# Attention and two feed-forward layers on one core: bank turns in the planner, offsets to the keys by section, zero products early

## The chip, the cores and the metric

One NeuronCore of a Trainium2 chip runs the whole program in one launch. The metric is device microseconds of that launch, the median of several runs. Five engines work side by side, each through its own list of instructions in order: TensorE (PE, matmuls), VectorE (DVE), ScalarE (ACT), GpSimd (POOL) and SyncE (SP), which here issues all DMA transfers.

## The reference

Attention within blocks of 64 tokens, then two feed-forward layers over 2304 tokens (512 to 2048 to 512 features each):

```python
def _attn_ref(q, k, v):          # (4, 8, 576, 64), chunks of 64
    scores = scale * np.matmul(q_c, k_c.transpose(0, 1, 2, 4, 3))
    scores = scores - np.max(scores, axis=-1, keepdims=True)
    attn = np.exp(scores)
    attn = attn / (np.sum(attn, axis=-1, keepdims=True) + 1e-09)
    return np.matmul(attn, v_c)
def _moe_ref(x, w_in, w_out, s, b):
    r = np.maximum(x @ w_in, 0.0)
    return (s * (r * r) + b) @ w_out
def _moe2_ref(x, w_in, w_out):
    h = x @ w_in
    return (np.maximum(h, 0.0) + np.log1p(np.exp(-np.abs(h)))) @ w_out
```

The weights arrive as float64, the rest as float32.

## The kernel before

**The stages.** (1) Attention over 18 tiles of 128 tokens by 512 features. (2) The first layer's input product, in 24 "quads": each is a 2 by 2 block product done with seven multiplications (p1 to p7, in the manner of Strassen and Winograd), for eight pairs of weight rows and three groups of six tiles. (3) The first layer's output product in six blocks of 16 steps. (4) The second layer's input product, again 24 quads. (5) Its output product, by the seven forms of the same scheme (`second_by_blocks`). All operands are split into a high and a low part (ACT makes the high part, DVE the low one), and each product is three matmuls of 384 columns: high by high, high by low, low by high.

**One tile of attention** (`attention`): DMAs of q, k in two halves, and v; scores on PE (L743) into a bank of kind `at`; the row maximum on DVE (L757); for the first six tiles the exponential on ACT in eight pieces with their sums (L767, after a negation at L779), for the others a subtraction on DVE (L789), one exponential on ACT (L802) and a sum on DVE (L810); a reciprocal on DVE (L820, L821); a multiplication on POOL (L827); turns on PE (L843); a copy out of the bank by ACT or DVE (L360, L362); values on PE (L862); then the result's forms, split into high and low (L515 on ACT, L524 on DVE), with subtractions on DVE and POOL (L502).

**A quad** (`quad`): p1, p6, p7 and p5 accumulate one after the other in one bank `ba`; between them ACT copies the partial sum as a seed into the banks of p2, p4 (`seed`, L948), ACT or DVE copies it out, and DVE subtracts (L502). So p6 waits for ACT's seed after p1, p7 for the copy after p6, and p5 for two readers of the same bank after p7, ACT's seed and DVE's subtraction. ACT finishes each output with L958. Products are L926.

**A block** (`block`, L1104): each of 16 steps has four accumulators (d = 0 to 3), each with three matmuls; the step's high and low parts lie in one of NGH = 4 buffers, so the split for step m+4 waits until all four accumulators of step m are done.

**Weights** come as float64 and are converted by `convert`: a DMA, five steps on DVE (L410, L440, L454, L468, L482) and one on ACT (L427) per half.

**What sets the order.** The program is first recorded as a list of `Op`s, each with the engines that may do it and their costs, a key (its due time in the author's scale), what it depends on, and which `Place`s (banks, buffers) it uses. `Work.order` then plays the list through: at each step it takes the engine and the operation that can start first and, among those that can start within 0.02, the one with the smallest key. What may go to two engines goes to the one that is found so. The instructions are written out in that order, and each engine executes its part strictly in it; semaphores between engines keep the dependences. PSUM has eight banks: two of kind `A`, three `S`, three `at`.

**The opening.** Before the planned list, DVE makes a zero tile, and five products of it (L1417) run on PE into the banks A and S.

## Time and profile before

| | |
|---|---|
| median of 3 runs | 820.55 us (819.38 to 821.25) |
| profiled execution | 818.22 us |
| its span, first to last instruction | 816.4 us |
| mean granted clock of PE | 0.993 of full |
| DMA | 180 MB, 221 GB/s on average |

The page gives busy shares of the engines over the span; as matmuls overlap one another, a busy PE need not run at its peak. The views by stretch tell how the shares change along the program: attention and the first quads lie in the first 100 us, the first layer's remaining quads up to about 258, the blocks up to about 460 with the first quads of the second layer from about 420, the quads up to about 630, and `second_by_blocks` from there to 812. In a timeline a row is one or more like instructions, with its start, its duration, the engine, the line and the tiles; in brackets stands the idle time of that engine just before it, and what ended it. A tile's name with its number left out (`at`, `S`, `last`) is a bank or a buffer of that kind.

### The profile page before, as it was taken

The page shows a single profiled execution, that of the slowest core. Times are in us where ns is not written, and L with a number is a line of the kernel's source. Part 1 is how long each engine was busy: PE and PEld are TensorE (multiplying, and loading weights), DVE is VectorE, ACT ScalarE, POOL GpSimd, SP SyncE. Part 2 cuts the span into 40 slices and gives each one's busy share as a digit, 9 for nine tenths or more (in the row PEclk, how much of TensorE's full clock was granted, in tenths as well). Part 3 has the DMA queues.
Part 4 walks back from the last instruction along what each step waited for, and adds up shares of the span by engine and source line. Part 5 has one row for each costly group of instructions (what it writes and reads, how often), then busy time and mean ns, then how long its engine had stood idle before and what let it go on. Part 6 is the DMA issues. An engine that isn't in the chain of part 4 may idle for free.

```text
span 816.4 us, 14526 instructions
## 1 busy us (share of the span) xinstructions
PE 788.6 (97%) x5117; PEld 771.9 (95%) x5117; DVE 637.4 (78%) x1170; ACT 507.4 (62%) x1080; POOL 144.7 (18%) x162
## 2 busy tenths in 40 slices
PE   5788999999999999999999999999999999999998
PEld 4677899999998999999999999999999999999997
DVE  5799899988856998989856696879675777777864
ACT  4655766666658796666566675565555565655543
POOL 4334422111110222222212230212010000000000
PEclk9799999999999999999999999999999999999999
DMA  8675368779759766778520037766778987678851
GB/s 246 202 200 170 127 188 285 240 244 286 241 192 349 287 226 199 257 218 256 199 83 35 15 141 265 240 230 206 280 237 268 348 351 245 220 255 285 265 193 59
DMA packets 80633, 180.27 MB, mean 221 GB/s; under 512 B 9008, under 2 KB 53040, under 8 KB 79664
## 3 DMA queue, kind: packets, MB, share of 16 engines
q1 hardware_dynamic: 80560, 179.34, 66.3%
q8 instruction: 40, 0.66, 0.3%
q14 instruction: 33, 0.27, 0.1%
HBM read 111.15 MB, written 68.16 MB: 220 GB/s over the span
## 4 chain that ended last, share of the span: by engine, by line
PE 88%; DVE 5%; ACT 2%; DMA 2%; issue 1%; SPq 1%; POOL 0%; DVEq 0%; ACTq 0%; POOLq 0%
PE at L926 19%; PE S L926 12%; PE S L1104 9%; PE at L1104 9%; PE S L1256 8%; PE at L1256 8%; PE A L926 8%; PE A L1104 6%; PE A L1256 5%; PE at L862 1%; DVE operands L524 1%; SPq L377 1%; PE at L743 1%; DVE mem L502 1%; DMA last<-in_k_dram 1%
## 5 line engine op out<-in xcount | busy, mean ns | idle before, releaser
L502 POOL TENSOR_TENSOR mem<-mem 128x256 f32<-128x256 f32 x120 | 109.7, 924 | 377.4 <-DVE mem L482 300.8
L524 DVE TENSOR_TENSOR operands<-mem,operands 128x384 fp32r<-128x384 f32 (+4 forms) x186 | 126.0, 698 | 53.9 <-ACT operands L515 52.2
L515 ACT CAST operands<-mem 128x384 fp32r<-128x384 f32 (+4 forms) x186 | 111.2, 620 | 59.2 <-PE at L1256 36.2
L524 DVE TENSOR_TENSOR operands<-last,operands 128x384 fp32r<-128x384 f32 (+2 forms) x184 | 111.2, 617 | 43.2 <-ACT operands L515 35.7
L515 ACT CAST operands<-last 128x384 fp32r<-128x384 f32 (+2 forms) x184 | 94.4, 527 | 75.7 <-PE A L1104 48.7
L926 PE MATMUL at<-operands 128*128 128x384 f32 x624 | 121.7, 337 | 0.2 <-ACT S L948 0.2
L926 PEld LDWEIGHTS at<-operands 128*128 128x128 f32 x624 | 109.6, 188 | 1.2 <-ACT S L948 1.1
L1104 PE MATMUL S<-operands 128*128 128x384 f32 x432 | 90.7, 335 | 1.2 <-ACT operands L515 0.9
L1104 PE MATMUL at<-operands 128*128 128x384 f32 x432 | 90.3, 334 | 0.0
L1256 PE MATMUL at<-operands 128*128 128x384 f32 x384 | 87.2, 334 | 0.0
L1256 PE MATMUL S<-operands 128*128 128x384 f32 x384 | 87.2, 334 | 0.0
L926 PE MATMUL S<-operands 128*128 128x384 f32 x420 | 82.7, 337 | 1.4 <-ACT S L948 1.4
L1104 PEld LDWEIGHTS S<-operands 128*128 128x128 f32 x432 | 76.2, 188 | 1.8 <-ACT operands L515 1.2
L958 ACT ACTIVATE mem<-S 128x384 f32<-128x384 f32 x104 | 51.1, 491 | 42.3 <-PE S L926 39.5
L1104 PEld LDWEIGHTS at<-operands 128*128 128x128 f32 x432 | 76.3, 188 | 0.0
L926 PEld LDWEIGHTS S<-operands 128*128 128x128 f32 x420 | 73.4, 188 | 1.8 <-ACT S L948 1.7
L1256 PEld LDWEIGHTS at<-operands 128*128 128x128 f32 x384 | 68.4, 188 | 0.0
L1256 PEld LDWEIGHTS S<-operands 128*128 128x128 f32 x384 | 68.4, 188 | 0.0
L502 DVE TENSOR_TENSOR mem<-mem 128x384 f32<-128x384 f32 (+1 forms) x108 | 59.4, 571 | 9.9 <-ACT mem L958 9.1
L926 PE MATMUL at<-last,operands 128*128 128x384 f32 x336 | 66.7, 336 | 0.5 <-ACT S L948 0.2
L1104 PE MATMUL A<-operands 128*128 128x384 f32 x288 | 65.3, 334 | 0.0
L926 PE MATMUL A<-operands 128*128 128x384 f32 x300 | 60.3, 340 | 1.1 <-ACT S L948 0.9
(79 smaller groups left out, 1199.9 us busy)
## 6 DMA issues: line engine op xcount, KB each, us to landing
mem<-in_w_dram SPq DMA_DIRECT2D x64, 512.0 KB, 4.6
summed<-mem SPq DMA_DIRECT2D x168, 192.0 KB, 2.4
mem<-summed SPq DMA_DIRECT2D x30, 768.0 KB, 5.0
hid<-mem SPq DMA_DIRECT2D x96, 192.0 KB, 3.7
last<-hid SPq DMA_DIRECT2D x24, 768.0 KB, 4.5
last<-summed SPq DMA_DIRECT2D x12, 768.0 KB, 5.2
mem<-forms SPq DMA_DIRECT2D x7, 1024.0 KB, 7.4
last<-in_q_dram SPq DMA_DIRECT2D x18, 256.0 KB, 4.2
```

Of the source, the lines that this page charges most:

```text
L377: lambda e: nc.sync.dma_start(out=out(), in_=in_()),
L502: lambda e: on(e).tensor_tensor(out=out(), in0=x(), in1=y(), op=op or ALU.subtract),
L515: lambda e: nc.scalar.copy(out=hi().bitcast(F32R), in_=x()),
L524: lambda e: nc.vector.tensor_tensor(out=lo().bitcast(F32R), in0=x(), in1=hi(), op=ALU.subtract),
L743: nc.tensor.matmul(out_[c * D : (c + 1) * D, pr], of("q")[:, pr * P + c * D : pr * P + (c + 1) * D], kb[:, :, pr, c, :], start=True, stop= ...
L862: nc.tensor.matmul(at(px)[y, x], of("v")[y, x], of("aT")[y, x], start=True, stop=True)
L926: nc.tensor.matmul(acc(dst)().rearrange("p (u c) -> p u c", u=GROUP), l[a], r[c], start=start and kk == 0 and x == 0, stop=kk == 1 and x == 2,
L958: lambda e: nc.scalar.activation(out=at(go), in_=acc(place)(), func=AF.Softplus if ph else AF.Relu),
L1104: nc.tensor.matmul(at(accs[d])[:, :N], l[a], r[c], start=m == 0 and z == 0, stop=m == NM - 1 and z == 2,)
L1256: nc.tensor.matmul(at(accs[d])[:, :N], l[a], r[c], start=i == 0 and y == 0, stop=i == NF - 1 and y == 2,)
```

## The change

`TUNE` is a table of 167 numbers that are added to the keys: by section and its turn ("block0 0 1 10": block, even step, group 0, half 1, step 10) and by the operation's place in a section ("attention.3": its fourth operation). `begin` names the section at each start. In `Work.order` an operation that uses a bank may not start before the last user of that bank, on another engine, has ended and handed over. Some costs are new (exponentials 0.3 instead of 0.4 a piece, scores 0.95 instead of 1.07), and the time up to which PE is counted at half speed goes from 16.25 to 7. `warmed` fills the gaps that PE has in the played-through order, up to the first use of the third S bank, with products of a zero tile `nought`, 512 columns each, into that bank; nobody reads them. There are 74 of them.

```diff
@@ TUNE, Place, Work @@
+TUNE = {
+    "attention 1": 3.5, "attention 14": 87, "attention 15": 11, "attention 16": -14, "attention 3": 6,
...
+}
-        self.kind, self.index, self.left = kind, None, 0
+        self.kind, self.index, self.left, self.last = kind, None, 0, None
+    BANKS = "A", "S", "at"
-    COLD = 16.2532
+    COLD = 7.0
+    def begin(self, part, *turn):
+        self.part, self.turn, self.nth = part, " ".join(map(str, (part, *turn))), 0
@@ add @@
+        kind, self.nth = f"{self.part}.{self.nth}", self.nth + 1
+        key += TUNE.get(self.turn, 0.0) + TUNE.get(kind, 0.0)
@@ order @@
+            for u in op.gives:
+                if u.kind in self.BANKS and u.last and u.last[1] != e:
+                    t = max(t, u.last[0] + self.AFTER[u.last[1]] + self.BEFORE[e])
...
+                u.last = op.end, e
+    IDLE = 0.22
+    def warmed(self, done, emit, kind, index):
+        t, out, unused = 0.0, [], True
+        for op in done:
+            unused = unused and all((u.kind, u.index) != (kind, index) for u in op.takes)
+            if op.on == "PE" and unused:
+                for x in range(int((op.start - t) / self.IDLE / (2 if op.start < self.COLD else 1))):
+                    out.append(Op({"PE": self.IDLE}, 0, [], [], [], emit, 0))
...
+                t = op.end
+            out.append(op)
+        return out
@@ attention, block (and the same in the other sections) @@
+        work.begin("attention", t)
-        o1 = add({"PE": 1.07}, key, scores, loads, [sc], r=sp("q", "k"))
+        o1 = add({"PE": 0.95}, key, scores, loads, [sc], r=sp("q", "k"))
-            o5 = add({"ACT": 8 * 0.4}, key, exps, [o3], [sc, *own], w=sp("e"))
+            o5 = add({"ACT": 8 * 0.3}, key, exps, [o3], [sc, *own], w=sp("e"))
+            work.begin(f"block{m % 2}", j, half, m)
@@ the end of the kernel @@
+        nc.vector.tensor_copy(out=nought, in_=zero[:, :P])
-        for op in done:
+        def idle(e):
+            x = bank["S"][2].rearrange("p (a b) -> p a b", b=P)
+            nc.tensor.matmul(x, nought, nought.unsqueeze(1).to_broadcast([P, KK, P]), start=True, stop=True)
+        for op in work.warmed(done, idle, "S", 2):
             op.emit(op.on)
```

What each engine is given to do is otherwise the same: the same products, splits, conversions and DMAs. Of the copies that may go to ACT or DVE, those of 512 columns are 12 on DVE and 18 on ACT before, 6 and 24 after.

The list of SP at the start, before (q, k, v and w are the inputs; k comes in two halves; `last_120` is the tile buffer of attention, `mem` the one for raw weights):

```order
L377 DMA last_120<-in_q_dram 128x512
L377 DMA last_120<-in_k_dram 64x512 x2
L377 DMA last_120<-in_v_dram 128x512
L377 DMA mem<-in_w_dram 128x1024 x2
L377 DMA last_120<-in_q_dram 128x512
L377 DMA last_120<-in_k_dram 64x512 x2
L377 DMA last_120<-in_v_dram 128x512
L377 DMA last_120<-in_q_dram 128x512
L377 DMA last_120<-in_k_dram 64x512 x2
```

and now (L446 is the load's line in the changed kernel):

```order
L446 DMA last_121<-in_q_dram 128x512
L446 DMA last_121<-in_k_dram 64x512 x2
L446 DMA mem<-in_w_dram 128x1024
L446 DMA last_121<-in_q_dram 128x512
L446 DMA last_121<-in_k_dram 64x512 x2
L446 DMA last_121<-in_q_dram 128x512
L446 DMA last_121<-in_k_dram 64x512 x2
L1405 DMA s_sb<-in_s_dram 128x1
L1406 DMA b_sb<-in_b_dram 128x1
L446 DMA mem<-in_w_dram 128x1024
L446 DMA last_121<-in_v_dram 128x512
```

The second half of the weights and v of the first tile went behind q and k of three tiles.

The list of PE at the start, before (`S_69` is the third S bank; L743 scores, L843 turns, L862 values):

```order
L1417 MATMUL S_69<-operands 128x512
L743 MATMUL at_70<-last_120 64x128 x8
L743 MATMUL at_71<-last_120 64x128 x8
L743 MATMUL at_72<-last_120 64x128 x8
L843 MATMUL at_70<-ident,last_120 128x128 x4
L862 MATMUL at_70<-last_120 64x64 x16
L743 MATMUL at_71<-last_120 64x128 x8
```

and now (L815, L915 and L934 are the same three, L1502 the zero products):

```order
L1498 MATMUL S_69<-operands 128x512
L1502 MATMUL S_69<-nought 128x512 x9
L815 MATMUL at_70<-last_121 64x128 x8
L1502 MATMUL S_69<-nought 128x512 x7
L815 MATMUL at_71<-last_121 64x128 x8
L1502 MATMUL S_69<-nought 128x512 x3
L815 MATMUL at_72<-last_121 64x128 x8
L1502 MATMUL S_69<-nought 128x512 x8
L915 MATMUL at_70<-ident,last_121 128x128 x4
L1502 MATMUL S_69<-nought 128x512 x4
L815 MATMUL at_71<-last_121 64x128 x8
L934 MATMUL at_70<-last_121 64x64 x16
```

Zero products stand between nearly all of the early steps, and the fourth scores went ahead of the first values.

The list of PE at the start of the first layer's blocks, before, where the last product of the quads (L926) is followed by the round of four accumulators (L1104), which then repeats to the end of the block:

```order
L926 MATMUL A_66<-operands 128x384 x6
L1104 MATMUL S_68<-operands 128x384 x3
L1104 MATMUL S_67<-operands 128x384 x3
L1104 MATMUL at_70<-operands 128x384 x3
L1104 MATMUL A_65<-operands 128x384 x3
L1104 MATMUL S_68<-operands 128x384 x3
```

and now, some twenty operations into the first block (L1179; x12 is one accumulator over four steps):

```order
L1179 MATMUL A_65<-operands 128x384 x9
L1179 MATMUL S_68<-operands 128x384 x3
L1179 MATMUL A_65<-operands 128x384 x3
L1179 MATMUL S_68<-operands 128x384 x9
L1179 MATMUL S_69<-operands 128x384 x12
L1179 MATMUL at_71<-operands 128x384 x12
L1179 MATMUL A_65<-operands 128x384 x3
L1179 MATMUL S_68<-operands 128x384 x3
```

The round is gone: one accumulator runs ahead over several steps, and the others follow it.

## Rows read from the trace of the kernel before

**Rows 1.** The page, part 1: busy time, share of the span, instructions.
```profile
PE 788.6 (97%) x5117; PEld 771.9 (95%) x5117; DVE 637.4 (78%) x1170; ACT 507.4 (62%) x1080; POOL 144.7 (18%) x162
```

**Rows 2.** Busy time of each engine by stretches of 40 us, columns as named.
```profile
core 0: us, PE busy (x) PEld busy (x) DVE busy (x) ACT busy (x) POOL busy (x), PEclk, DMA share, GB/s
0.00:40.00 40.00, 25.67 (x291) 20.55 (x293) 26.53 (x59) 23.09 (x109) 15.45 (x25) 0.87 0.75 222
40.00:80.00 40.00, 35.06 (x533) 30.01 (x530) 39.03 (x79) 22.75 (x39) 17.93 (x20) 1.00 0.67 194
80.00:120.00 40.00, 39.27 (x355) 37.04 (x354) 35.78 (x65) 29.05 (x58) 15.45 (x16) 1.00 0.46 147
...
320.00:360.00 40.00, 40.00 (x232) 40.00 (x232) 35.07 (x67) 26.87 (x55) 10.20 (x12) 1.00 0.76 238
```

**Rows 3.** Timeline, block loop: start, duration, engine, line, operation [idle before it <-releaser].
```profile
420.72 0.68 PE L1104 MATMUL A<-operands 128*128 128x384 f32 x3
...
421.24 1.20 PE L1104 MATMUL S<-operands 128*128 128x384 f32 x6
421.43 0.51 ACT L515 CAST operands<-last 128x384 fp32r<-128x384 f32 x1 [1.57 <-PE A L1104]
421.98 0.56 DVE L524 TENSOR_TENSOR operands<-last,operands 128x384 fp32r<-128x384 f32 x1 [1.52 <-ACT operands L515]
```

**Rows 4.** Timeline of PE after attention, places with waits.
```profile
90.98 1.15 PE L862 MATMUL at<-last 64*64 64x64 f32 x32
...
95.95 1.32 PE L926 MATMUL A<-operands 128*128 128x384 f32 x6 [0.50 <-ACT S L948]
...
466.47 1.32 PE L926 MATMUL S<-operands 128*128 128x384 f32 x6 [1.39 <-ACT S L948]
...
501.92 1.31 PE L926 MATMUL at<-last,operands 128*128 128x384 f32 x6 [0.19 <-ACT S L948]
```

**Rows 5.** Timeline of PE in the first 28 us.
```profile
3.26 1.48 PE L1417 MATMUL S<-operands 128*128 128x512 f32 x3
...
5.47 1.97 PE L743 MATMUL at<-last 128*64 128x128 f32 x16 [0.73 <-DMA last<-in_k_dram]
...
11.45 1.98 PE L743 MATMUL at<-last 128*64 128x128 f32 x16 [4.00 <-DMA last<-in_k_dram]
...
14.17 1.98 PE L743 MATMUL at<-last 128*64 128x128 f32 x16 [0.74 <-DMA last<-in_k_dram]
...
19.05 1.09 PE L743 MATMUL at<-last 128*64 128x128 f32 x16
...
24.41 1.97 PE L743 MATMUL at<-last 128*64 128x128 f32 x16
```

**Rows 6.** Stretches of 2 us, with the granted clock.
```profile
24.00:26.00 2.00, 2.00 (x26) 1.86 (x22) 0.86 (x3) 1.87 (x13) 1.57 (x2) 0.50 0.81 259
```

**Rows 7.** Timeline of ACT, pieces of the exponentials of tiles 0, 2 and 5.
```profile
9.08 0.30 ACT L767 ACTIVATE last<-at,mx 128x64 f32<-128x64 f32 x1
...
11.11 0.34 ACT L767 ACTIVATE last<-at,mx 128x64 f32<-128x64 f32 x1
...
22.41 0.36 ACT L767 ACTIVATE last<-at,mx 128x64 f32<-128x64 f32 x1
...
35.59 0.35 ACT L767 ACTIVATE last<-at,mx 128x64 f32<-128x64 f32 x1
```

**Rows 8.** Timeline of DVE, two of the reciprocals.
```profile
37.46 0.20 DVE L821 RECIPROCAL sm<-sm 128x8 f32<-128x8 f32 x1
...
86.53 0.20 DVE L821 RECIPROCAL sm<-sm 128x8 f32<-128x8 f32 x1
```

**Rows 9.** DVE's instructions by form: busy us, mean ns, idle before.
```profile
L482 DVE SCALAR_TENSOR_TENSOR mem<-mem 128x512 f32<-128x512 f32 x64 | 43.9, 686 | 1.2
...
L362 DVE COPY last<-at 128x512 f32<-128x512 f32 x6 | 4.1, 678 | 0.1
```

**Rows 10.** Timeline of ACT, a seed.
```profile
253.50 0.46 ACT L948 COPY S<-at 128x384 f32<-128x384 f32 x1 [0.26 <-DVE mem L502]
```

More of the change, by code (lines that the diff above doesn't have):

```diff
@@ L113 @@
     BYTES = 300e3
-    COLD = 16.2532
+    COLD = 7.0
     def __init__(self):
         self.ops = []
+        self.part, self.turn, self.nth = "", "", 0
+    def begin(self, part, *turn):
+        self.part, self.turn, self.nth = part, " ".join(map(str, (part, *turn))), 0
     def add(self, engines, key, emit, deps=(), uses=(), size=0, after=()):
+        kind, self.nth = f"{self.part}.{self.nth}", self.nth + 1
+        key += TUNE.get(self.turn, 0.0) + TUNE.get(kind, 0.0)
         op = Op(engines, key, [d for d in deps if d is not None], [], list(uses), emit, size)
@@ L133, in add @@
             u.left += 1
+        op.kind, op.turn = kind, self.turn
         self.ops.append(op)
@@ L205, in order @@
         return done
+    IDLE = 0.22
[6 more added lines that the diff above has]
+                    out.append(Op({"PE": self.IDLE}, 0, [], [], [], emit, 0))
+                    out[-1].on, out[-1].start = "PE", t + x * self.IDLE
+                    out[-1].end = out[-1].start + self.IDLE
+                t = op.end
+            out.append(op)
+        return out
 def dve(n, fast=False, pointers=0, port=True):
@@ L277, in block_attention_two_layers @@
         ident = const.tile([P, P], F32, name="ident")
+        nought = const.tile([P, P], F32R, name="nought")
         s_sb = const.tile([P, 1], F32, name="s_sb")
@@ L534, in weights1 @@
     def weights1(ph, i, key):
+        work.begin("weights1", ph, i)
         wf, wp = Place("wf"), Place("w1")
@@ L552, in weights2 @@
     def weights2(ph, i, key):
+        work.begin("weights2", ph, i)
         x = ((AT_XO, 3) if ph == 0 else (AT_S2, 1))
@@ L843, in turned @@
                 nc.tensor.transpose(at(pt)[:, c], of("e")[:, c], ident)
-        o8 = add({"PE": 0.44}, key, turned, [o7], [pt, *own], r=sp("e"))
+        o8 = add({"PE": 0.48}, key, turned, [o7], [pt, *own], r=sp("e"))
         o9 = add(
@@ L866, in attention @@
         key += 0.3
-        o10 = add({"PE": 1.07}, key, values, [o9, load_v], [px], r=sp("aT", "v"))
+        o10 = add({"PE": 1.05}, key, values, [o9, load_v], [px], r=sp("aT", "v"))
         got = lambda: two(at(px))
@@ L889, in forms_held @@
     def forms_held(u, key):
+        work.begin("held", u)
         (xe, ce), (xd, cd) = held[2 * u], held[2 * u + 1]
@@ L905, in quad @@
     def quad(ph, i, j, w, keys, kinds):
+        work.begin(f"quad{ph}", i, j)
         wp, w_done = w
@@ L1142, in forms_of @@
     def forms_of(j, key):
+        work.begin("forms_of", j)
         spans = [(ybuf[2 * j + x], KK4) for x in range(2)]
@@ L1154, in second_by_blocks @@
     def second_by_blocks(ph, t0):
+        work.begin("second", "start")
         V2, G2, GH = 512, 4 * N, 2 * N
@@ L1168, in weights @@
         def weights(n, key, gone=None):
+            work.begin("weights", n)
             wp = Place("w1")
@@ L1227, in second_by_blocks @@
             for i in range(NF):
+                work.begin(f"second{i % 4}", n, j, i)
                 key = t + i * T
@@ L1282, in second_by_blocks @@
             }[n]
+            work.begin("sums2", n, j)
             for d in range(2):
```

34 rows, old and new, of the table TUNE are left out of this document.

## The prediction

> **What bounds the kernel now.** I read the busy shares first: TensorE (PE) is busy 788.6 of 816.4 us [rows 1]. Then the 40 us stretches: from 320 to 360 and in most later ones PE is full, so nothing that other engines save there can be seen in the time; the stretches with a loss are the first two, with 25.67 and 35.06 of 40, and a little at 80 to 120. In 40 to 80 VectorE (DVE) is busy 39.03 of 40: there DVE sets the pace, and attention is what it works on [rows 2].
>
> The work of PE is fixed: 4176 product matmuls at 0.173 us each, the distance of 421.24 from 420.72 for three [rows 3], 724 us; and 18 tiles of attention at 1.09 (scores), about 0.4 (turns) and 1.05 (values), 45 us. 816.4 less 769 leaves 47 us. The last values of attention start at 90.98 and end at 92.1 [rows 4], with 13 of the 696 six-matmul products done; by then PE has done 13.5 + 45 us of work, so 33 us of the 47 are lost before that point. Another 4.1 us is the tail after the last matmul, and some 10 are left for the 720 us between. A change of order can win from the 33 and a little from the 10.
>
> Why the first part is slow is seen in three views. The scores of tiles 1 and 2 wait 4.00 and 0.74 us for k [rows 5]. PE's clock fell in the early gaps: it was granted 0.50 from 24 to 26 us, the 1.2 GHz level, after a stretch in which PE was busy less than half of the time, and the scores at 24.41 take 1.97 us where those at 19.05 took 1.09 [rows 5, 6]. (For the first 14 us the view grants 1.00, but scores there took 1.97 too; the durations tell the level there.) And ScalarE (ACT) does the first six tiles' exponentials in eight pieces each: the first set begins at 9.08 and ends about 11.5, the third starts its last piece at 22.41, the sixth at 35.59 [rows 7]. After that DVE never rests: the sixth reciprocal of its own order is at 37.46, the eighteenth at 86.53, 49.1 us for twelve tiles [rows 8].
>
> **The change, part by part.**
>
> (a) The loads. Ahead of tile 1's last k stood 2.3 MB (q, k, v of tile 0, two halves of weights, q, k); now 1.5 MB. Ahead of tile 2's k stood 3.1 MB; now 2.0. At the 222 GB/s of the first stretch [rows 2] that is 3.5 and 4.8 us earlier: k is there at about 8 instead of 11.45, and about 9.5 instead of 14.17. What pays is v of tile 0 and the second weight half, which land later; v is wanted only after the first turns (16 us in the trace), the weights after 45 us. I cost that at nothing.
>
> (b) The zero products: 74 in 17 places, of 512 columns. At the rate of the five that already open the program, 1.48 us for three [rows 5], one takes 0.49; at twice the clock 0.22 by halving with the fixed part. Nine stand before the first scores. The opening five end at 4.74, so the nine end between 6.8 and 9.1; the k wait ended at 5.47. I take 7.9: the first tile is 2.4 us later, but its scores then take 1.09 instead of 1.97, which makes 9.0 against 7.44, 1.5 us late. All 74 come to 16.3 us at 0.22. PE had 14.8 us of waits (13 of them, the first at 5.47, the longest at 11.45 [rows 5]) and about 7 us of slow work before 60 us, so they fit, but only just: the work up to the first product and its three zeros adds to 4.7 + 16.3 + 25.9 (11 scores, 9 turns, 9 values, 1 product) = 47 us, a floor for that point.
>
> (c) The early chain of ACT. DVE does the first maximum (0.69), then two steps of a weight conversion (1.1) before it scales the maximum, so the first exponentials start near 11.0 instead of 9.08. But sets two and three now follow with no other ACT work between and with their scores long done: at 2.45 us each they end at 18.3 instead of 22.8. From there ACT's order to the end of set six holds three more sets (7.4), three copies and three small casts (3.4), two casts of 1024 columns (2.1) and a conversion step and one cast more (1.4): 32.6, against 36.0 now. With the first scores at 6.8 it is 31.5; were k late, 34. So the sixth reciprocal comes 3.4 us earlier, with 2 to 5 as bounds.
>
> (d) DVE's share. Six copies of 512 columns move from DVE to ACT (12 before, 6 now; 0.68 each, [rows 9]). Between the sixth and the eighteenth reciprocal DVE's order now has three copies less (-2.0), one subtraction of scores and one of forms less (-1.1), and four steps of a conversion more (two at 0.69 [rows 9], two estimated at 0.4, +2.2): -0.9. ACT has room: busy 22.75 of 40 [rows 2]. So the eighteenth reciprocal, and with it the last values, come 3.4 + 0.9 = 4.3 us earlier. And 14 products stand before the last values instead of 13: another 1.0. Since DVE works from the sixth reciprocal on without rest, its cover is whole; if PE's zeros or a bank push a turn or a value past its place, DVE waits in order and each wait is added. I take **-5.3** from (a) to (d), bounds -8 (DVE also fills its early idle time) and 0 (each place of zeros late).
>
> (e) The later waits. After the last values seven waits of PE are visible, the first of 0.50 at 95.95, the largest of 1.39, the last of 0.19 at 501.92, together 3.83 us [rows 4]. Five of them end with ACT's copy out of a bank, the seed of the next product. One thing that delays a seed is seen at 253.50: ACT waits 0.26 us for DVE, which reads the same bank [rows 10]. In the order of before, six of the 48 pairs p7 to p5 of the quads, which have that pair of readers between them, stand one product apart; now none stands under two. In exchange more of the 96 pairs with one reader (p1 to p6, p6 to p7) stand at most one product apart (42 instead of 26), which the 0.48 us of a seed and its hand-overs just fit. I take **-1.4**, bounds -3.8 and +2.
>
> (f) The block loop (the six blocks at L1104). Before, the four accumulators of a step go round; the step's operands sit in one of four buffers, and between the last use of a buffer and the first use of what replaces it PE has twelve operations of 0.52 us, 6.2 us. Now one accumulator runs ahead by up to four steps and the others follow. Counting in PE's order, 18 of 92 refills have only three operations (1.56 us) and 40 at most four. A refill takes, from the last use at 420.72 + 0.52: ACT starts at 421.43, DVE at 421.98 and is done 0.56 later [rows 3], 1.3 us in all, and the second matmul needs the DVE half, 0.17 after the first. So 1.56 covers it by about 0.35, if ACT and DVE are free on the spot. In 320 to 360 they are busy 26.87 and 35.07 of 40 [rows 2] with conversions between. This loop is full before, so it can only lose. I take **+0.4**, that is 0.01 a refill, since most find the engines free; bounds 0 and +8 (0.2 us at each of 40).
>
> The sum: -5.3 - 1.4 + 0.4 = -6.3. Against the profiled execution of 818.22 us this gives 811.9 (span 810.1). That execution was 2.3 us under the median of the runs, 820.55; on the median the forecast is **814.2**.
>
> **The rivals.**
>
> 1. The early gain is eaten (818.5 to 821). Zeros and real work share one queue, and a zero that is late holds up what is behind it; if 17 places lose 0.25 us each, that is 4.3 us, and (a) to (d) shrink to -1. For it: the opening five already end at 4.74, so the nine zeros run past k. Against: DVE, not PE, paces 40 to 90, and half a microsecond on PE there is covered. 818.5.
>
> 2. Slower: the block loop. If ACT or DVE is behind by more than the 0.35 us of cover, PE waits at the 40 tight refills; with 0.3 us each that is +12 where I took +0.4, and the time is 826. It decides from an average of 0.17 us a refill, where it has eaten all 6.7 us of the rest. For it: DVE at 35 of 40, and a step of a conversion of 0.69 may stand ahead. Against: the cover is positive in each of them, and a wait once paid shifts all engines alike.
>
> 3. More than forecast: PE fills the early part to its floor (47 us at the first product, where before had 49.45 for the start of its first and less attention done) and the later waits go wholly: -8 - 3.8 = 808.5.
>
> 4. The zeros do not hold the clock. Then each takes 0.49 and 74 take 20 us more, and it ends near 835. Rows for it: the five opening products, whose operands are zeros too, did not make the next scores fast [rows 5]; but they were followed by a gap. Against: the clock rose in the trace after PE had run scores, turns and values with little between, as from 14.17 to 19.05 [rows 5]. The Trainium skill, "TensorE: Matmul & The Clock Gate", section "HAM oscillation", names idle gaps of some length as what lowers the clock; by that rule the short gaps here (1.33 us at most between 16 and 27 us) would not have lowered it and most of the zeros would buy nothing but still cost no more than 0.22 each. The trace decides against that part: it fell to 0.50 after just such gaps [rows 6].
>
> **How the numbers follow.** Forecast (within 3 us of 814.2) 0.53; rival 1, 0.15; rival 2, 0.14; rival 3, 0.15; rival 4, 0.03. This kernel's measurement tells about 0.2%, 1.6 us, from no change. Faster: the forecast, rival 3, and a third of rival 1: 0.73. Within: half of rival 1 and a little of rival 2, 0.10. Slower: the rest, 0.17. The range runs from 808.5 (rival 3) to 820.5 (rival 1's far side); what lies above, the most of rivals 2 and 4, is about 0.15, what lies below 0.05.
>
> **What would show it.** In the profile of the changed kernel: the second and third scores start before 10.5 and 12.5 us; the granted clock is 1.00 in every stretch after 20 us; the sixth tile's exponentials end by 33; the eighteenth reciprocal stands at 82 and the last values at 87; waits of PE after that sum to under 3 us; stretches inside the blocks show PE full, with no wait for ACT or DVE at the casts. Wrong would be: first scores after 10, DVE idle between 40 and 80, a row of short waits of PE on the casts in the block loop, or a clock below 1.00.

## The result, and the profile after

The changed kernel takes 808.76 us in the median (807.26 to 809.31, five runs), the kernel before on the same chip 819.38 (817.78 to 821.25, five runs): a ratio of 0.9863, with a 95% interval of 0.9847 to 0.9879. It is faster by 10.6 us. The forecast had the sign, and its range holds the time, but the step was too small: it named -6.3, from the 820.55 of three runs to 814.2, and 814.2 is only 5.2 below the 819.38 of all five. The profiled executions are 807.7 us with a span of 805.9, and 818.22 with 816.4: 10.5 us apart, and those are what is taken apart below.

Part 1 of the page of the changed kernel, which answers to [rows 1]:

```profile
PE 797.4 (99%) x5191; PEld 780.1 (97%) x5191; DVE 637.8 (79%) x1166; ACT 510.1 (63%) x1085; POOL 140.6 (17%) x162
```

Its stretches of 40 us, as in [rows 2]:

```profile
core 0: us, PE busy (x) PEld busy (x) DVE busy (x) ACT busy (x) POOL busy (x), PEclk, DMA share, GB/s
0.00:40.00 40.00, 37.54 (x428) 28.88 (x430) 29.95 (x65) 26.39 (x116) 17.40 (x27) 1.00 0.87 251
40.00:80.00 40.00, 39.61 (x576) 33.80 (x573) 38.63 (x80) 24.64 (x45) 19.20 (x20) 1.00 0.60 173
80.00:120.00 40.00, 40.00 (x283) 39.32 (x282) 35.28 (x62) 29.48 (x60) 13.24 (x14) 1.00 0.51 170
320.00:360.00 40.00, 40.00 (x233) 39.95 (x232) 34.57 (x60) 30.05 (x60) 10.92 (x12) 1.00 0.80 247
```

PE looks full from the start, but in the first two rows a part of that is filler, the 74 zero products. DVE's 38.63 of 40 in the second row points at what still sets the pace there (experiment 7).

PE's timeline in the first 14 us, which answers to [rows 5]:

```profile
4.53 3.02 PE L1502 MATMUL S<-nought 128*128 128x512 f32 x9
7.48 1.09 PE L815 MATMUL at<-last 128*64 128x128 f32 x16
8.50 1.89 PE L1502 MATMUL S<-nought 128*128 128x512 f32 x7
10.32 1.09 PE L815 MATMUL at<-last 128*64 128x128 f32 x16
11.35 0.96 PE L1502 MATMUL S<-nought 128*128 128x512 f32 x3
12.24 1.09 PE L815 MATMUL at<-last 128*64 128x128 f32 x16
```

The scores of the first three tiles take 1.09 each, and the second and third no longer wait for k.

The end of attention, in the timelines of ACT (last piece of the sixth tile's exponentials), DVE (the sixth and the eighteenth reciprocal of its order) and PE (the last values); these answer to [rows 7], [rows 8] and [rows 4]:

```profile
33.25 0.35 ACT L839 ACTIVATE last<-at,mx 128x64 f32<-128x64 f32 x1
...
34.60 0.20 DVE L893 RECIPROCAL sm<-sm 128x8 f32<-128x8 f32 x1
...
83.26 0.20 DVE L893 RECIPROCAL sm<-sm 128x8 f32<-128x8 f32 x1
...
87.22 1.15 PE L934 MATMUL at<-last 64*64 64x64 f32 x32
```

All waits of PE after that, by what was waited for, with their sum, number and longest:

```profile
PE at L1179 <- ACT operands L584: 0.8, 1, 0.8
PE at L1000 <- ACT S L1022: 0.4, 1, 0.4
PE A L1000 <- DVE A L571: 0.4, 1, 0.4
PE at L1179 <- DVE operands L593: 0.2, 1, 0.2
```

Four are left, 1.7 us together, where seven with 3.83 were seen before. By this view 2.1 us were won there; by the starts of the matmuls it is 6.0, with 0.3 given back in the blocks.

**Where the 10.5 us came from.** From the start times of all 4176 product matmuls each kernel's time can be split without asking any view what a wait is: a start that follows the one before by more than 0.173 us (the distance in [rows 3]) has lost the difference. "Early" is the start of the last matmul of attention less 0.173 us for every product matmul done before it; the other columns are the time lost after that, by the place in the span: the quads up to 240 us, the entry into the blocks (240 to 275), the blocks (to 425), the second layer's quads. The last stage loses less than 0.3 in every kernel. With 4176 x 0.1733 = 723.7 us each line adds up to the start of the last matmul.

| kernel | early | quads | entry | blocks | quads 2 | last matmul |
|---|---|---|---|---|---|---|
| before | 78.4 | 3.5 | 2.2 | 0.0 | 4.3 | 812.2 |
| changed | 73.6 | 0.5 | 1.5 | 0.3 | 2.0 | 801.6 |
| changed, no zero products | 73.4 | 0.5 | 1.7 | 0.3 | 2.0 | 801.6 |
| changed, offsets all 0 | 79.7 | 3.5 | 3.6 | 0.0 | 4.0 | 814.5 |
| changed, rule of turns out | 80.6 | 9.7 | 6.6 | 6.9 | 10.0 | 837.5 |
| before, rule of turns in | 81.2 | 4.1 | 2.5 | 0.0 | 4.0 | 815.5 |
| before, six pairs spaced | 79.8 | 3.9 | 2.7 | 0.0 | 4.5 | 814.7 |
| changed, loads back | 78.6 | 0.5 | 1.5 | 0.3 | 2.0 | 806.7 |
| the same without zero products | 75.6 | 1.7 | 1.8 | 0.4 | 2.0 | 805.2 |
| changed, ten copies back | 77.8 | 0.5 | 4.0 | 0.3 | 2.0 | 808.3 |
| before, zero products in | 77.3 | 3.5 | 2.3 | 0.0 | 4.3 | 811.1 |
| before, new order of loads | 78.9 | 4.0 | 2.3 | 0.0 | 4.3 | 813.2 |
| changed, early offsets only | 73.6 | 0.5 | 4.6 | 0.0 | 4.0 | 806.5 |
| changed, late offsets only | 81.9 | 3.3 | 4.7 | 3.6 | 2.0 | 819.3 |

The first two lines: 4.8 us early, 6.0 in the later losses (3.0 in the quads, 0.7 at the entry, 2.3 in the second layer's quads), and 0.3 given back in the blocks. The early stage of like orders differed by 1 us and more between executions (78.4 and 79.8 in two with the same order there), so single steps of that size in the first column are not read; each line is one execution.

**Why the waits view showed so little.** PE's timeline of before at one of these places, with the two instructions of ACT and DVE that release it:

```profile
98.16 3.69 PE L926 MATMUL A<-operands 128*128 128x384 f32 x18
101.70 1.20 PE L926 MATMUL S<-operands 128*128 128x384 f32 x6
...
99.41 0.48 ACT L948 COPY S<-A 128x384 f32<-128x384 f32 x1
...
99.92 0.56 DVE L502 TENSOR_TENSOR mem<-A,mem 128x384 f32<-128x384 f32 x1 [0.20 <-ACT S L948]
```

No bracket stands at PE. But 18 matmuls at 0.173 are 3.12 us, and the next row starts after 3.54: 0.42 are lost inside the row. The row holds p7 (98.16 to 99.20), one product between, and p5. After p7 ACT copies the seed (99.41 to 99.89), then DVE, which was idle 0.20 for it, reads the same bank until 100.48, and p5 starts at 100.53 instead of 100.24. A matmul's recorded end lies some 0.17 behind the next start, so up to that much of a gap shows nowhere, and the second matmul after a stall starts another 0.11 late. The start at 501.92 in [rows 4] shows 0.19 and costs 0.47.

The same view of the changed kernel, twelve matmuls and the next row:

```profile
92.57 2.24 PE L1000 MATMUL A<-operands 128*128 128x384 f32 x12
94.65 1.20 PE L1000 MATMUL S<-operands 128*128 128x384 f32 x6
```

2.08 us from start to start, 12 x 0.173: nothing lost. The p7 that starts at 92.57 has two products behind it, and its p5 starts on time at 95.69. After 92 us, all six pairs p7 to p5 with one product between were stalled in the kernel before, 2.53 us in all, and none of nine with two. In the changed kernel none has one, 25 have two, and none of these is stalled. Of the pairs with one reader (p1 to p6, p6 to p7) at one product apart, 1 of 24 stalled before and none of 39 now.

The pairs are a quarter of the 10.0 us that the first line of the table loses after attention. The largest single loss of the quads, 1.67 us at 466.47 [rows 4], is another thing. In ACT's timelines of before and of the changed kernel:

```profile
464.25 1.28 ACT L958 ACT_TABLE_LOAD   x1
...
465.93 0.48 ACT L948 COPY S<-at 128x384 f32<-128x384 f32 x1
```

```profile
458.04 1.28 ACT L1032 ACT_TABLE_LOAD   x1
...
459.86 0.46 ACT L1022 COPY S<-at 128x384 f32<-128x384 f32 x1
```

Ahead of the second layer's first activation ACT loads its table for 1.28 us, and the seed that PE waits for stands behind that load. Before, one product stood between the p7 of that seed and the p4 that needs it; now three stand between p7 and p5, the first product to need it, and the loss there is 0.70 (460.38), with 0.65 more at the p3 behind it (463.10).

### The profile page after: what moved, and what is told of

Same layout as the page of the kernel before. It is cut to its first block, busy times and chain, and to the rows that moved or that the text cites. A ratio compares the mean times of both kernels' runs of the same rounds, so it can differ in the third digit from the quotient of the medians.

```text
span 805.9 us, 14677 instructions
## 1 busy us (share of the span) xinstructions
PE 797.4 (99%) x5191; PEld 780.1 (97%) x5191; DVE 637.8 (79%) x1166; ACT 510.1 (63%) x1085; POOL 140.6 (17%) x162
## 4 chain that ended last, share of the span: by engine, by line
PE 95%; DVE 3%; ACT 1%; issue 0%; POOL 0%; ACTq 0%; POOLq 0%; DVEq 0%
PE at L1000 20%; PE S L1000 13%; PE at L1179 9%; PE S L1179 9%; PE A L1000 9%; PE S L1335 8%; PE at L1335 8%; PE A L1179 6%; PE A L1335 5%; PE S L1502 2%; PE at L934 2%; PE at L815 1%; PE at L915 1%; DVE operands L593 1%; ACT last L839 0%
## 5 line engine op out<-in xcount | busy, mean ns | idle before, releaser
L571 POOL TENSOR_TENSOR mem<-mem 128x256 f32<-128x256 f32 x120 | 104.8, 883 | 377.6 <-DVE mem L551 279.9
L1000 PE MATMUL at<-operands 128*128 128x384 f32 x624 | 120.1, 336 | 0.4 <-ACT S L1022 0.4
L1335 PE MATMUL at<-operands 128*128 128x384 f32 x384 | 87.2, 334 | 0.0
L1335 PE MATMUL S<-operands 128*128 128x384 f32 x384 | 87.2, 334 | 0.0
L1179 PE MATMUL at<-operands 128*128 128x384 f32 x432 | 84.5, 335 | 0.9 <-ACT operands L584 0.8
L1000 PE MATMUL S<-operands 128*128 128x384 f32 x420 | 83.6, 336 | 0.0
L1179 PE MATMUL S<-operands 128*128 128x384 f32 x432 | 83.1, 334 | 0.0
L1179 PEld LDWEIGHTS at<-operands 128*128 128x128 f32 x432 | 75.5, 188 | 1.9 <-ACT operands L584 1.1
L1179 PEld LDWEIGHTS S<-operands 128*128 128x128 f32 x432 | 75.6, 188 | 0.0
L1000 PEld LDWEIGHTS S<-operands 128*128 128x128 f32 x420 | 73.6, 188 | 0.3 <-issue 0.2
L1000 PE MATMUL A<-operands 128*128 128x384 f32 x300 | 60.2, 339 | 0.4 <-DVE A L571 0.4
L1000 PEld LDWEIGHTS at<-last,operands 128*128 128x128 f32 x336 | 58.8, 188 | 0.0
```

The lines of the kernel that those rows point to most:

```text
L571: lambda e: on(e).tensor_tensor(out=out(), in0=x(), in1=y(), op=op or ALU.subtract),
L1000: nc.tensor.matmul(acc(dst)().rearrange("p (u c) -> p u c", u=GROUP), l[a], r[c], start=start and kk == 0 and x == 0, stop=kk == 1 and x == 2,
L1179: nc.tensor.matmul(at(accs[d])[:, :N], l[a], r[c], start=m == 0 and z == 0, stop=m == NM - 1 and z == 2,)
L1335: nc.tensor.matmul(at(accs[d])[:, :N], l[a], r[c], start=i == 0 and y == 0, stop=i == NF - 1 and y == 2,)
```

## The experiments

Each is the changed kernel or the one before with one thing undone or done alone. "Before" in a ratio is the kernel before, run in the same session on the same chip.

**1. The zero products out, the order kept.**

```diff
-        for op in work.warmed(done, idle, "S", 2):
+        for op in done:
```

> The changed kernel in exactly its order, without the 74 zero products (nobody reads them). Theory A, the order does it and the zero products only hold the clock: the granted clock falls below 1 somewhere between 15 and 40 us, scores there take 1.97 instead of 1.09, the last values come 1 to 3 us later than 87.2, and the time is 810 to 812 against 808.8; the loss of the 4092 matmuls after the last values stays at about 4.3 us. Theory B, the zero products are most of the early gain: last values at 90 or later, 813 or more. Theory C, they are ballast that PE is paced by until 60 us: 806 to 808.

Measured: 810.02 us, 0.9883 of before (0.9856 to 0.9911). The profiled execution, the fastest of four, has a span of 805.9, the same as with them. PE's second and third scores and its last values, and the first stretch of 40 us:

```profile
9.93 4.08 PE L815 MATMUL at<-last 128*64 128x128 f32 x32 [2.62 <-DMA last<-in_k_dram]
...
86.98 1.15 PE L934 MATMUL at<-last 64*64 64x64 f32 x32
```

```profile
0.00:40.00 40.00, 27.12 (x375) 21.56 (x377) 29.14 (x65) 26.82 (x116) 17.13 (x27) 1.00 0.87 249
```

PE waits 2.62 us for k and does two tiles' scores at half the rate (4.08 for 32 matmuls), yet the last values start at 86.98, not after 87.22. In this execution all of it is under the cover of ACT and DVE, and the granted clock stays at 1.00 from 18 us on without a single zero product. In the other three it did not hold throughout: their mean clock was 0.993 to 0.998, and they took 809.78 to 810.91, while with zero products all five read 0.999 and took 807.26 to 809.31. So the zero products buy nothing where the clock holds without them; whether they are worth the 0.2% between the two ratios, which lies inside their intervals, is not shown.

**2. All offsets zero.** The rule, the zero products (placed anew) and the new costs stay.

```diff
-        key += TUNE.get(self.turn, 0.0) + TUNE.get(kind, 0.0)
+        key += 0.0
```

> The changed kernel with every offset of the table at nought: the bank turns in the planner, the new costs and zero products (placed anew) stay. Theory A, the turns remove the stalls after attention and the table orders the start: stalls after the last values under 6 us against 10 before and 4.3 with the table, last values about 90, time 812 to 816. Rival, the table does nearly all: within 2 us of the kernel before, 817 to 821. Rival, the table does nearly nothing: 808 to 811.

Measured: 820.40 us, 1.0015 (1.0001 to 1.0028), span 818.8. Without the table there is no gain at all; every column of losses is back at before's size, and the entry to the blocks is worse.

**3. The rule of turns out, the table kept.**

```diff
-    BANKS = "A", "S", "at"
+    BANKS = ()
```

> The changed kernel with the rule of the bank turns taken out of the planner, table kept (made for the rule, so the order is another one in many places). Theory A, the turns keep the third link of a quad at two products: without the rule places with one product between p7 and p5 come back and each costs about 0.4 us; losses after the last values 8 us or more, 812 to 818. Rival, the table does it whatever the rule: 808 to 811.

Measured: 843.17 us, 1.0307 (1.0268 to 1.0346), span 841.5. The same offsets in a planner without the rule make another order, and it is the slowest of all: 33 us lost behind the early part. The table pays only in the planner with the rule. (The granted clock fell once, to 0.50 from 270 to 273; what each of its stalls comes from was not taken apart.)

**4. The rule alone, in the kernel before.**

```diff
+            for u in op.gives:
+                if u.kind in self.BANKS and u.last and u.last[1] != e:
+                    t = max(t, u.last[0] + self.AFTER[u.last[1]] + self.BEFORE[e])
...
```

> The kernel before with the bank turns in the planner alone: no table, no zero products, old costs. Theory A: the losses after the last values fall from 10 us to 5 to 7, attention stays as it was (last values 90 to 93): 814 to 817 against 819.4. Rival, the rule alone moves nothing: 819 to 820. Rival, a rule without the table makes the order worse: above 821.

Measured: 819.59 us, 1.0014 (0.9997 to 1.0031). The rule in the planner is worth nothing by itself: the order that it makes is no better.

**5. The six close pairs moved apart, by hand, in the order of before.** Where one product stands between p7 and p5, the one behind p5 goes ahead of it.

```diff
...
+            if at - line.index(p7) == 2:
+                done.remove(line[at + 1])
+                done.insert(done.index(p5), line[at + 1])
...
```

> The kernel before with one edit: at the six places where p5 stands one product behind p7, the product after p5 goes ahead of it, so that two stand between. Nothing else in the order changes. Theory A, two readers in turn (ACT's seed, DVE's subtraction) need more than the 1.04 us of one product: all six stalls (0.29 to 0.36 at p5's first matmul and 0.1 at its second, 2.5 us in all) go, the losses after the last values fall from 10.0 to 7.5 us, and the time by 2 to 2.5 us. Rival: the stall only moves to the next link (p3 after p5 is one product nearer): less than 0.7 us.

Measured: 820.49 us, 1.0022 (1.0007 to 1.0036): no gain. The stalls at p5 are gone, 0 of 15 pairs with two products between. But PE's timeline has them elsewhere:

```profile
103.76 1.21 PE L938 MATMUL A<-operands 128*128 128x384 f32 x6
105.10 2.20 PE L938 MATMUL S<-operands 128*128 128x384 f32 x11
...
258.95 1.33 PE L938 MATMUL A<-operands 128*128 128x384 f32 x6 [0.73 <-DVE A L512]
```

From 103.76 to 105.10 are 1.34 us for six matmuls (1.04), a loss of 0.30 with no bracket, and at 258.95 it is 0.89. Both are p3, the quad's next link after p5, which now stands too close behind it: eight such pairs have at most one product between, before five. Five of the eight stall, 3.7 us in all; before it was one, with 0.41. The stall went one link down the chain. (The changed kernel has seven such pairs, and of these only the one at 463.10 stalls, behind the table load, so the count alone does not decide at that link; what else does was not settled.)

**6. v of tile 0 and the second weight half back to their early places**, beside the first weight load, in SP's list of the changed kernel.

```diff
...
+    for op in (v0, half):
+        done.remove(op)
+    done.insert(done.index(first), v0)
+    done.insert(done.index(first) + 1, half)
```

> The changed kernel with two loads of SP put back to where they stood: v of tile 0 ahead of the first weights, the second weight half right behind the first. Theory A, the early chain hangs on k of tiles 1 and 2: their scores start about 2 us later (12 and 14 instead of 10.3 and 12.2), the sixth tile's exponentials end 1 to 2 us later than 33.6, the last values 1 to 2 later than 87.2, time 809.8 to 811. Rival, ACT and DVE cover it: less than 0.4 us.

Measured: 812.59 us, 0.9920 (0.9899 to 0.9941), span 811.0. The last values come 5.0 us later, more than expected. PE's timeline:

```profile
8.97 1.91 PE L1509 MATMUL S<-nought 128*128 128x512 f32 x7
13.88 1.83 PE L815 MATMUL at<-last 128*64 128x128 f32 x16 [3.00 <-DMA last<-in_k_dram]
15.64 1.65 PE L1509 MATMUL S<-nought 128*128 128x512 f32 x3
17.21 1.20 PE L815 MATMUL at<-last 128*64 128x128 f32 x16
...
92.25 1.15 PE L934 MATMUL at<-last 64*64 64x64 f32 x32
```

PE waits 3.00 for k, the granted clock is 0.50 from 14.1 to 17.5, so the scores after the gap take 1.83 instead of 1.09, and then PE still has to do the zero products that were counted out for a gap that isn't there any more: three of them took 1.65, against 0.96 in the changed kernel.

**7. Ten copies' engines put back** (eight of them to DVE, two to ACT), the changed order kept.

```diff
+    back = {(0, 13): "DVE", (2, 11): "DVE", (3, 11): "DVE", (4, 11): "ACT", (5, 11): "DVE", (7, 12): "ACT"}
+    back |= {(8, 14): "DVE", (10, 14): "DVE", (14, 12): "DVE", (17, 14): "DVE"}
...
```

> The changed kernel with the ten copies of attention that changed engine put back (eight to DVE, two to ACT, each in its place of the order): DVE does six copies of 0.68 us more. Theory A, DVE paces attention: the last values come 2.5 to 4 us later than 87.2, time 811 to 813. Rival, the copies are not on the path: less than 1 us.

Measured: 813.22 us, 0.9932 (0.9912 to 0.9951). DVE's sixth and eighteenth reciprocals of its order:

```profile
36.07 0.20 DVE L893 RECIPROCAL sm<-sm 128x8 f32<-128x8 f32 x1
...
87.76 0.20 DVE L893 RECIPROCAL sm<-sm 128x8 f32<-128x8 f32 x1
```

1.5 and 4.5 us later than in the changed kernel (34.60, 83.26), and the last values 4.2. Each copy of 0.68 on DVE goes into the end of attention nearly whole. DVE paces that stage, as the prediction read it. The entry to the blocks lost 2.5 more besides: PE waited 1.16 and 0.15 us there, and the granted clock fell to 0.50, in a stretch of 2 us:

```profile
256.00:258.00 2.00, 2.00 (x8) 2.00 (x8) 2.00 (x5) 2.00 (x6) 0.00 (x0) 0.50 1.05 398
```

**8. The zero products alone, in the order of before** (`nought`, `idle` and `warmed` added; 67 of them).

```diff
...
-        for op in done:
+        for op in work.warmed(done, idle, "S", 2):
```

> The kernel before in its own order, with zero products in the gaps of PE that its planner sees. Theory A (the changed kernel without them lost nothing, so they do not matter): the clock stays at its upper level from 10 us on, the early scores, turns and values take half the time, but DVE and the loads pace, so the last values move by less than 1.5 us and the time is 817 to 820. Rival, the clock was what held the start back: last values 3 us or more earlier, under 816. Rival, zero products late in the queue hold up the real ones: above 821.

Measured: 818.54 us, 0.9998 (0.9984 to 1.0012). In the profiled executions the mean granted clock went from 0.993 to 1.000 (over all runs of that session 0.989 to 0.998 without them, 0.997 to 1.000 with them), so they do hold it; the last values came 1.1 us earlier, no more than the spread of that stage, and the time does not show it.

**9. Only the early offsets:** attention, the copies held from it, the first quad, the first weights; the rest 0.

```diff
+        early = (self.part in ("attention", "held", "quad0") or self.turn.startswith(("weights1 0", "weights2 0")))
-        key += TUNE.get(self.turn, 0.0) + TUNE.get(kind, 0.0)
+        key += TUNE.get(self.turn, 0.0) + TUNE.get(kind, 0.0) if early else 0.0
```

> The changed kernel with the table's entries of attention, the held forms, the first layer's quads and weights alone; those of the blocks and of the second layer at nought. Theory (each part of the table pays in its own stage): first values and first quads as in the changed kernel (last values near 88 at their end, 2 to 2.5 us lost in the first layer's quads), but about 4 us lost in the second layer's quads against 2.0: 810.5 to 812. Rival, all of the gain is early: 808 to 809.5. Rival, the parts only work together: 815 or more.

Measured: 813.03 us, 0.9919 (0.9894 to 0.9943), span 810.4. The whole early gain is there, and the 3.0 us of the first quads too. What is missing against the changed kernel is 3.1 at the entry to the blocks and 2.0 in the second layer's quads. The entry, in PE's and DVE's timelines and in stretches of 2 us:

```profile
249.22 1.32 PE L1001 MATMUL A<-operands 128*128 128x384 f32 x6 [1.16 <-DVE A L572]
251.48 0.45 PE L1180 MATMUL S<-operands 128*128 128x384 f32 x1 [0.94 <-ACT operands L585]
...
247.40 1.29 DVE L594 TENSOR_TENSOR operands<-last,operands 128x512 fp32r<-128x512 f32 x2
248.61 0.56 DVE L572 TENSOR_TENSOR A<-at,mem 128x384 f32<-128x384 f32 x1
```

```profile
248.00:250.00 2.00, 0.84 (x5) 0.78 (x5) 2.00 (x5) 2.00 (x6) 0.00 (x0) 1.00 1.09 411
250.00:252.00 2.00, 1.00 (x5) 0.40 (x3) 2.00 (x5) 2.00 (x5) 0.00 (x0) 0.94 1.00 396
252.00:254.00 2.00, 1.65 (x5) 1.65 (x6) 2.00 (x5) 2.00 (x5) 0.00 (x0) 0.50 1.03 396
254.00:256.00 2.00, 2.00 (x10) 2.00 (x9) 1.18 (x3) 1.14 (x4) 0.00 (x0) 0.70 1.05 412
```

DVE splits forms of the first block (247.40) ahead of a subtraction of the last quads (248.61) that PE waits for. Then the first block's operands come late, and PE, idle for more than half of 4 us, is granted 0.50: seven starts in a row are 0.32 apart, 1.0 of the 3.1 us. In the changed kernel the waits there are 0.78 and 0.15 and the clock stays at 1.00.

**10. Only the late offsets** (the condition of 9 turned round).

```diff
+        key += 0.0 if early else TUNE.get(self.turn, 0.0) + TUNE.get(kind, 0.0)
```

> The changed kernel with the complement: entries of the blocks and of the second layer alone. Same theory: start and first quads as without the table (last values at 92, 6 to 7 us lost in the first layer's quads), 2 to 2.5 us lost in the second layer's quads: 816.5 to 819. Rival, together only: 820 or more.

Measured: 822.24 us, 1.0038 (1.0020 to 1.0057). The second layer's quads are as good as in the changed kernel (2.0); everything ahead of them is as before or worse, the blocks with 3.6. The two halves of the table don't add up: +2.7 us and -6.5 against -10.6 together. Why the entry needs both was not taken apart.

**11. The new order of the first loads alone, in the kernel before.**

```diff
+    sp = [op for op in done if op.on == "SP"]
+    last = sp[12]
+    for op in (sp[5], sp[3], sp[9]):
+        done.remove(op)
+        done.insert(done.index(last) + 1, op)
+        last = op
```

> The kernel before with the changed kernel's order of the first loads alone (the second weight half and v of tiles 0 and 1 behind k of tile 2); DVE, ACT and PE keep their order. Theory A, the loads pay only with an order of DVE and ACT that fits them: here DVE and ACT have the second half of the weights ahead of the second tile's maximum and exponentials, so they wait for it in order and the early k helps nothing: last values within 1.5 us of 92 or later, 818 to 822. Rival, the loads are the whole of the early gain: last values 3 us or more earlier, under 816.

Measured: 818.54 us, 0.9998 (0.9981 to 1.0015). PE and ACT in the first 16 us:

```profile
8.90 3.45 PE L743 MATMUL at<-last 128*64 128x128 f32 x32 [1.34 <-DMA last<-in_k_dram]
...
12.45 0.63 ACT L427 ACTIVATE mem<-mem 128x512 int32<-128x512 int32 x1 [0.80 <-DVE mem L410]
15.39 0.32 ACT L767 ACTIVATE last<-at,mx 128x64 f32<-128x64 f32 x1 [2.31 <-DVE mx L779]
```

The second scores start at 8.90 instead of 11.45, but the second tile's exponentials wait until 15.39: in DVE's and ACT's old orders the steps of the second weight conversion stand ahead of their maximum, DVE waits 0.91 at 11.99 for those weights, which now come later, and ACT's step of the conversion waits for DVE. An earlier load pays only in an order of ACT and DVE that goes for it.

**12. Experiment 6 without the zero products.**

```diff
-        for op in work.warmed(done, idle, "S", 2):
+        for op in done:
```

> The kernel with the two loads put back (last values at 93.2 instead of 88.2) without its zero products. Theory A, part of those 5.0 us is the zero products, which keep their number behind a late k and pace PE: without them the last values come at 90.5 to 92, time 810 to 811.5. Rival, the chain of ACT and DVE alone carries the whole delay: 93 again, 812 to 813. Rival, the clock falls in the long gap and costs more than the zero products did: 94 or later.

Measured: 810.95 us, 0.9908 (0.9873 to 0.9944), span 809.5. The last values of PE:

```profile
89.26 1.15 PE L934 MATMUL at<-last 64*64 64x64 f32 x32
```

They start 3.0 us before those of experiment 6 and 2.0 after those of the changed kernel. So of the 5.0 us that the old loads cost up to there, 2.0 are the late k itself, and 3.0 the zero products that stand in PE's list behind it. Of the 3.0, half is lost again in the quads and at the entry (the two lines in the table), so the two spans are 1.5 us apart, and the medians 1.6; the two ratios alone don't separate them, their intervals overlap.

No version ran faster than the changed kernel; the one without zero products is within the noise of it. The new costs in the planner were not undone by themselves.

## Why the prediction was right and where it was wrong

**What failed is the size of (e).** It took -1.4 with -3.8 as the most that could be won; it was -6.0. The step that failed is the one that read seven waits and their sum of 3.83 [rows 4] as all that was lost behind attention. The starts lose 10.0 us there in the kernel before: 5.8 at the seven places themselves, the rest where the view shows nothing. The prediction had the figure in its hands: its own budget left "some 10" us for the 720 between, and it did not ask why its waits came to 3.83.

The mechanism that it named, two readers in turn behind p7, is there, down to the six pairs that stand one product apart: all six stalled, 0.42 each, 2.5 us in all, of which the waits view shows two, with 0.4. But it is a quarter of what was lost, and experiment 5 adds that it could not have been won alone: spaced by hand, the close pairs hand the stall to p3. The price that the prediction saw for it, more pairs of one reader at one product apart, was none: such pairs just fit, as it wrote, and none of the 39 behind attention stalled. What it had not named is ACT's table load ahead of the seed at 466.47 (1.39 in the view, 1.67 by the starts, 0.70 and 0.65 now). Most of the rest, 0.4 to 0.8 us at single places of the first quads, went with the early offsets (experiment 9); which of them did it was not taken apart.

**(a) to (d), -5.3: measured -4.8, by the stated path.** The second and third scores start at 10.32 and 12.24 (under 10.5 and 12.5 were stated). The sixth tile's exponentials end at 33.6 where 32.6 was worked out; the sixth reciprocal came 2.9 us earlier, not 3.4, and the stretch from it to the eighteenth shrank by 0.4 (49.1 to 48.66), not 0.9. The last values start 3.8 earlier, not 4.3, and 14 products stand before them, as worked out. Two readings in this sum were off, and partly cancel. k of the second tile was not there at 8: without zero products PE waits for it until 9.93 (experiment 1). And ACT was ahead at the third set, which starts its last piece at 17.08, but then lost 2.0 us in two waits for DVE's scaled maxima ahead of the fifth and sixth sets, where the sum has ACT working without a pause. Experiment 7 shows that DVE's copies set the stretch between the reciprocals (51.7 with them back); experiments 6, 11 and 12 that the loads are needed but pay only with the new order of ACT and DVE.

**(b), the zero products.** They fit, as the sum of 47 us said they could, and the clock read 1.00 behind them. The first exponentials start at 10.43, where 11.0 was worked out. The prediction folded the worth of the fast scores into (a) to (d); experiment 1 has slow scores and the same end. **Rival 4** fell: from 11.35 on three zero products take 0.96, not 1.48, and the time does not hang on them.

**Rival 1** (zeros hold up real work) fell for the changed kernel, where loads are on time: the first scores start at 7.48, and the last values are within 0.3 us of those without zeros (87.22 and 86.98); experiments 6 and 12 show its mechanism at work, 3.0 us at the last values, as soon as one is late.

**(f), +0.4: measured +0.3.** One place shows in PE's timeline of the changed kernel:

```profile
308.69 0.97 PE L1179 MATMUL at<-operands 128*128 128x384 f32 x3
309.50 1.72 PE L1179 MATMUL A<-operands 128*128 128x384 f32 x9
```

0.81 us from start to start for three matmuls (0.52). All other refills are on time, the 18 with three operations between them too, so **rival 2** fell: a cover of 0.35 us was enough with DVE at 34.57 of 40 from 320 to 360.

**Rival 3** gave 808.5, and that is nearly the time, by luck, since the division is another: it wanted -8 early and -3.8 later, and the kernel did -4.8 and -6.0.

**Cause, as far as it is shown.** The gain is made by the table within the planner with the rule (2, 3, 4): early offsets give the 4.8 and the 3.0 in the first quads (9), late ones by themselves the 2.3 in the second layer's quads (10), and at the entry to the blocks both are needed (9, 10). Which offsets within each half matter was not tested.

## What to carry to other kernels

Where an engine is nearly full, take its lost time from the distances between starts, not from a view of its waits: here 3.8 us were shown and 10.0 lost, and the term for them came out 4.6 too small. Where a budget leaves more than a view shows, look for the rest before setting a bound. In an order written out in advance, moving one close pair apart can hand the stall to the next link (experiment 5), and a load that comes earlier gained nothing until the engines behind it took it earlier (11); try such moves as one order, not one by one. Filler that keeps an engine busy cost nothing that could be seen while its gaps were real, and 3.0 us up to the last values when a load was late (6, 12), since the list is in order.

## What the runs showed of the hardware that was not expected

- A short stall can be paid for once more by the clock. Behind two waits of 1.16 and 0.94 us (experiment 9), with PE busy 0.84 and 1.00 in two stretches of 2 us, the grant fell to 0.50, the 1.2 GHz level, and seven starts in a row were 0.32 apart instead of 0.173: 1.0 us on top. The Trainium skill, "TensorE: Matmul & The Clock Gate", section "HAM oscillation", puts the fall down to one idle gap longer than any of these; experiment 9 and [rows 6] disagree, since there it came after shorter gaps with matmuls between them. Experiment 7 has the same fall, and experiment 10 (0.61 and 0.54 from 260 to 264). The waits alone don't tell when: in experiment 2 PE waited 1.34, 0.95 and 0.35 us at the entry, and the grant stayed at 1.00. It did so in the kernel before, with less waiting:

```profile
258.30 0.45 PE L1104 MATMUL S<-operands 128*128 128x384 f32 x1 [0.85 <-ACT operands L515]
259.06 1.14 PE L1104 MATMUL S<-operands 128*128 128x384 f32 x5 [0.31 <-DVE operands L524]
```

- Holding the clock in the early part was worth nothing by itself in the order of before: from 0.993 to 1.000 in the mean of the profiled executions (experiment 8), 0.9998 in time.
- ACT's load of an activation table took 1.28 us ahead of the second layer's first activation, and a seed behind it made PE's largest single stall in the quads of the kernel before (1.67 us at 466.47).
- Two readers of one PSUM bank, ACT then DVE, took 1.28 us from p7's last matmul's end by distance (99.20) to DVE's end (100.48), and p5 started at 100.53. The Trainium skill, "PSUM — Partial Sum Buffer", section "PSUM bank collisions raise a hardware error", says that accesses of a bank by different engines are to be kept apart; the trace agrees (DVE idle 0.20 until ACT's copy ends), and gives the price: one product of 1.04 between is too short by 0.29, two of 2.08 were enough in all 34 pairs seen.
